# Polysketch attention and a mixture of experts: the query stage in a written order, with its work spread anew over the engines

## The chip, the core and the metric

The kernel runs on one core of a Trainium2 chip. A core has TensorE (matrix multiplies, into the PSUM memory of eight banks), VectorE and ScalarE (element by element, both read SBUF and PSUM), GpSimd (element by element in SBUF only) and SyncE, whose queue issues most of the DMA transfers. Each engine runs its own instructions in order. The metric is the device time of one execution in microseconds. In the profile's tables PE is TensorE, PEld its weight loads, DVE VectorE, ACT ScalarE, POOL GpSimd, SP SyncE.

## The reference

Attention with a polynomial sketch, 4 batches, 4 heads, 1088 positions, 32 dimensions, is followed by a two-level mixture of experts on the 4352 tokens of 128 dimensions:

```python
def phi(x):                                   # r = 8: 64 features per head
    a = einsum('rd,bhsd->bhsr', S1, x)
    b = einsum('rd,bhsd->bhsr', S2, x)
    return einsum('bhsi,bhsj->bhsij', a, b).reshape(*x.shape[:-1], r * r)
q_p, k_p = phi(q), phi(k)
kv  = einsum('bhsf,bhsd->bhfd', k_p, v)       # numerator's matrix
num = einsum('bhsf,bhfd->bhsd', q_p, kv)
den = einsum('bhsf,bhf->bhs', q_p, k_p.sum(2))[..., None] + 1e-06
x   = (num / den)                             # -> (4352, 128), heads side by side
g_logits = x @ w_group                        # argmax: group, then expert in it
e_logits = x_g @ w_expert[g]
out = g_w * e_w * (relu(x @ w1[g, e]) @ w2[g, e])
```

The denominator can come close to zero and the choice of an expert hangs on the quotient, so the kernel computes the denominator much more exactly than in fp32.

## The kernel before

**Stages.** First the k stage, batch by batch: k is cut into four bf16 slices, their products give the Gram matrix of k, which small steps (`refine`) turn into the matrix M; beside it the features of k times v give KV. Then the query stage, the part that is changed: nine units of four token tiles of 128 (the last has two). Then the routing stage, on VectorE for the most part: gates from the logits `lg`, and a sort of the tokens by expert, whose slots are computed by the matmuls `slot`. Last the expert stage, blocks of 128 tokens gathered by indirect DMA, two layers of fp32 matmuls, scattered to the output.

**The order of work.** Outside the expert stage a scheduler of the framework places the instructions on each engine; only the expert stage stands in `manual_schedule`, which keeps the written order on every engine. A pool's tile with `bufs=n` has n buffers, and an instruction that writes a buffer waits for the last readers of its former content.

**A unit of the query stage before** has two halves, written one unit apart:

- `features` (line 386 on). VectorE cuts q into four bf16 slices `qs` (`grid`, line 113: add a large constant and subtract it again, which rounds), GpSimd subtracts each slice from the rest `rq` (line 398). The four `products` per tile (line 139) multiply slice i by the first 4 - i orders of M (256, 192, 128, 64 columns) and add by order into PSUM `py`, two tiles at a time in two buffers. VectorE turns the four orders into three parts a1, a2, a3 (seven operations of 128 elements for each half of the unit), and GpSimd multiplies the parts of the two factors (eleven operations of 128 elements, lines 426 and 429) into `pr_`. Separately TensorE computes `ab` from q in fp32 (line 450, four tiles of 512 columns in three buffers, each in two instructions), ScalarE copies one factor to `ra` (line 453), and VectorE multiplies the other by it to `qp` (line 123).
- `quotient` (line 458 on). VectorE sums `pr_` to the denominator and takes the reciprocal `rec`; TensorE multiplies `qp` with KV into `pnum` (line 477, 64 columns for each pair of heads, 16 instructions in a unit); VectorE multiplies by `rec` to `xt`, which goes to DRAM as `x_d`. Then `xt` is transposed on TensorE (`px`, line 488), copied by ScalarE, multiplied with the router's weights `wr` (`pl`, line 493, 20 columns) and copied to `lg` (line 495).

## Time and profile before

| | |
|---|---|
| median of 3 runs | 468.19 us (466.86 to 469.38) |
| the profiled execution | 467.57 us, span 465.7 us, mean granted TensorE clock 0.773 |
| TensorE busy | 362.4 us (78%), weight loads 299.8 us |
| VectorE, GpSimd, ScalarE busy | 248.1, 205.9, 64.7 us |
| HBM | 29.00 MB read, 4.85 MB written |

The span is the time between the first and the last recorded instruction of the profiled execution; its own time holds some 1.9 us more. Busy time is summed over the whole span, over stages with different limits, so the tables by stage count for more. The clock is a share of 2.4 GHz: 0.50 is 1.2 GHz. Matmuls that follow each other overlap, so the time of one is read from the distance between the starts, not from its duration.

### The profile page before, as it was taken

How to read it: one execution, taken by the hardware profiler on the slowest of the kernel's cores; microseconds unless marked ns; L12 is line 12 of the kernel's file. 1: busy time of each engine (PE TensorE's matmuls, PEld its weight loads, DVE VectorE, ACT ScalarE, POOL GpSimd, SP SyncE). 2: the span in 40 equal slices, each digit the busy share in tenths (PEclk: the TensorE clock that was granted, in tenths of full speed). 3: DMA queues.
4: the chain of work that ended last, by engine and by line, in shares of the span. 5: the costliest groups of instructions: out<-in, count | busy, mean ns of one | idle time of the engine just before them, and what ended most of it. 6: DMA issues, size and time to landing. Idle time of an engine off the chain costs nothing.

```text
span 465.7 us, 6912 instructions
## 1 busy us (share of the span) xinstructions
PE 362.4 (78%) x2445; PEld 299.8 (64%) x2445; DVE 248.1 (53%) x750; ACT 64.7 (14%) x96; POOL 205.9 (44%) x248
## 2 busy tenths in 40 slices
PE   0428996972689998999959206599999999999970
PEld 0416884861253463774838106499999999999970
DVE  8698446176774575665563799323333333333320
ACT  1000000000101111111101100032222232222220
POOL 0472255100173675654653000436665556566660
PEclk9999597995665556555555556689999999999995
DMA  7991087029600000000001000101111111111120
GB/s 300 394 291 28 23 265 226 1 62 414 247 2 1 23 24 0 23 24 23 23 1 45 12 1 0 30 15 36 31 38 34 30 34 36 33 39 34 34 38 3
DMA packets 16101, 33.95 MB, mean 73 GB/s; under 512 B 2229, under 2 KB 6593, under 8 KB 16064
## 3 DMA queue, kind: packets, MB, share of 16 engines
q1 hardware_dynamic: 13376, 28.35, 17.9%
q0 software_dynamic: 2688, 5.12, 4.2%
q8 instruction: 22, 0.36, 0.3%
q14 instruction: 15, 0.12, 0.1%
HBM read 29.00 MB, written 4.85 MB: 73 GB/s over the span
## 4 chain that ended last, share of the span: by engine, by line
PE 54%; DVE 20%; issue 11%; POOL 9%; DMA 2%; ACT 0%; SPq 0%; POOLq 0%; DVEq 0%; ACTq 0%
PE ph L693 12%; PE py L699 11%; PE ab L450 9%; PE pnum L477 5%; PE py L139 4%; PE pg L305 3%; PE pl L493 3%; POOL xg L670 3%; PE slot L642 2%; POOL rk L300 2%; DVE ks L113 2%; PE px L488 1%; POOL rq L398 1%; DVE top_p_k L91 1%; DVE kp L326 1%
## 5 line engine op out<-in xcount | busy, mean ns | idle before, releaser
L693 PE MATMUL ph<-xb,w1b 128*128 128x128 f32 x656 | 82.5, 281 | 0.0
L693 PEld LDWEIGHTS ph<-xb,w1b 128*128 128x128 f32 x656 | 79.3, 198 | 0.0
L699 PE MATMUL py<-W,hT 128*128 x640 | 78.0, 275 | 0.0
L704 POOL DMA_INDIRECT out_dram<-yo,idx_s x40 | 53.2, 1331 | 49.3 <-DVE yo L702 31.4
L699 PEld LDWEIGHTS py<-W,hT 128*128 128x128 f32 x640 | 74.6, 192 | 0.0
L670 POOL DMA_INDIRECT xg<-x_d,idx_g x44 | 43.7, 992 | 52.2 <-DVE idx_s L521 39.1
L695 ACT ACTIVATE hT<-ph 128x1024 f32<-128x1024 f32 x41 | 42.0, 1023 | 143.2 <-PE ph L693 135.2
L450 PE MATMUL ab<-qT,SR 64*128 64x512 f32 (+1 forms) x72 | 54.8, 1007 | 0.1
L305 PE MATMUL pg<-ks 128*128 128x512 bf16 (+3 forms) x144 | 33.3, 349 | 16.8 <-DVE ks L113 16.8
L702 DVE TENSOR_SCALAR yo<-py,wslot 128x128 f32<-128x128 f32 x40 | 14.0, 351 | 59.9 <-PE py L699 52.5
L139 PEld LDWEIGHTS <-qs 128*128 128x128 bf16 (+1 forms) x144 | 14.9, 137 | 34.7 <-DVE qs L113 12.0
L680 DVE COPY w1b<-W 128x1024 f32 x42 | 29.4, 700 | 8.3 <-DVE yo L702 5.0
L139 PE MATMUL py<-M,qs 128*128 128x256 bf16 (+6 forms) x144 | 25.1, 323 | 9.3 <-DVE qs L113 6.7
L398 POOL TENSOR_TENSOR rq<-qT,qs 128x512 f32<-128x512 f32 (+1 forms) x9 | 10.1, 1123 | 49.0 <-DVE qs L113 42.4
L477 PE MATMUL pnum<-KV,qp 128*128 128x64 f32 (+1 forms) x144 | 30.7, 395 | 0.0
L477 PEld LDWEIGHTS pnum<-KV,qp 128*128 128x128 f32 (+1 forms) x144 | 28.8, 304 | 2.3 <-issue 1.5
L687 DVE COPY xb<-pt 128x128 f32<-128x128 f32 x42 | 12.2, 291 | 33.8 <-PE pt L686 29.6
L113 DVE TENSOR_SCALAR qs<-rq,CQ 128x512 bf16<-128x512 f32 (+1 forms) x27 | 17.1, 632 | 21.9 <-POOL rq L398 21.9
L305 PEld LDWEIGHTS <-ks 128*128 128x128 bf16 x144 | 14.7, 112 | 21.4 <-issue 18.6
L300 POOL TENSOR_TENSOR rk<-rk,ks 128x1152 f32<-128x1152 f32 x8 | 19.6, 2446 | 19.2 <-DVE ks L113 7.1
L450 PEld LDWEIGHTS ab<-qT,SR 64*128 64x128 f32 x72 | 16.7, 299 | 12.4 <-issue 7.0
L300 POOL TENSOR_TENSOR rk<-kn,ks 128x1152 f32<-128x1152 f32 x4 | 10.1, 2522 | 29.1 <-DVE pw L100 16.3
(313 smaller groups left out, 491.6 us busy)
## 6 DMA issues: line engine op xcount, KB each, us to landing
W<-in_w_dram SPq DMA_DIRECT2D x4, 2048.0 KB, 12.4
kn<-in_kn_dram SPq DMA_DIRECT2D x4, 576.0 KB, 5.3
kT<-in_kT_dram SPq DMA_DIRECT2D x4, 576.0 KB, 6.5
vn<-in_vn_dram SPq DMA_DIRECT2D x4, 576.0 KB, 3.9
qT<-in_qT_dram SPq DMA_DIRECT2D x4, 544.0 KB, 11.6
x_d<-xt SPq DMA_DIRECT2D x8, 256.0 KB, 2.3
xg<-x_d,idx_g POOLq DMA_INDIRECT x44
out_dram<-yo,idx_s POOLq DMA_INDIRECT x40
```

The lines of the kernel that those rows point to most:

```text
L113: nc.vector.tensor_scalar(out=out, in0=in_, scalar1=c, scalar2=c, op0=ALU.add, op1=ALU.subtract)
L139: nc.tensor.matmul(out(i), lhsT=left(i), rhs=right(NS - i), start=(i == 0), stop=(i == NS - 1), skip_group_check=True)
L300: nc.gpsimd.tensor_tensor(out=r, in0=rest, in1=ks[:, i], op=ALU.subtract)
L305: nc.tensor.matmul(pg[:, i:NS, :], lhsT=ks[:, i, c, :], rhs=ks[:, 0:NS - i, c, :], start=(c == 0 and i == 0), stop=(c == SC - 1 and i == N ...
L450: nc.tensor.matmul(ab[x][:, 0:w], lhsT=SR[rows, x].rearrange("p a x y -> p (a x y)"), rhs=qf[rows], start=True, stop=True)
L477: nc.tensor.matmul(pnum[r0:r0 + n, c, 64 * pr:64 * pr + 64], lhsT=qp[:, pr, cols], rhs=KV[:, b, pr, :], start=True, stop=True)
L670: nc.gpsimd.indirect_dma_start(out=xg(b), out_offset=None, in_=x_d, in_offset=bass.IndirectOffsetOnAxis(ap=idx_g[:, b:b + 1], axis=0))
L680: nc.vector.tensor_copy(out=w1b(b), in_=W1[:, ds(ex[b], 1), :].rearrange("p o f -> p (o f)"))
L693: nc.tensor.matmul(ph(b)[:, f], lhsT=w1b(b)[:, 128 * f:128 * f + 128], rhs=xb(b), start=True, stop=True)
L695: nc.scalar.activation(out=hT(b), in_=ph(b), func=ACT.Relu)
L699: nc.tensor.matmul(py(b), lhsT=hT(b)[:, f], rhs=W2[:, ds(ex[b] * FC + f, 1), :].rearrange("p o d -> p (o d)"), start=(f == 0), stop=(f == ...
L704: nc.gpsimd.indirect_dma_start(out=out, out_offset=bass.IndirectOffsetOnAxis(ap=idx_s[:, b:b + 1], axis=0), in_=yo(b), in_offset=None, bou ...
```

## The change

The query stage is written anew, under `manual_schedule`: each engine issues in the written order, in which the stages of three units interleave.

- **Slices of q.** The first two slices come from ScalarE (`act_grid`: two ACTIVATEs with a per-partition bias, +c and -c), the third is a ScalarE copy, the fourth is GpSimd's last subtraction. The slices of units 0 to 2 are issued ahead of the first matmul, those of later units two or three units ahead.
- **Orders.** One PSUM tile `py` for four tiles of tokens, in one buffer, with three orders in place of four (the last two added by TensorE). Seven matmuls per tile in place of four, 640 columns as before. M's layout has the factor ahead of the head.
- **Parts.** ScalarE rounds the first (`parts_a`), VectorE does five operations on the whole unit (256 elements per partition), into one tile `pp`.
- **Products.** GpSimd has one add and two wide multiplications, VectorE reduces the seven products to three sums.
- **spread, copy_a, features.** The four `ab` tiles have a buffer each; ScalarE copies one factor into `qp`, and VectorE multiplies in place.
- **Logits.** After the k stage, KVX is built per batch: KV beside KV times the router's weights (a transpose and a matmul on TensorE, copies on ScalarE). The numerator then has 52 columns per head, 104 per instruction, and carries the logits; `divide` multiplies both parts by `rec` and sums the heads' logits into `lg` on VectorE. The transposes `px`, the matmuls `pl` and their two ScalarE copies are gone.
- **Smaller.** wr is loaded ahead of qT, M is cleared by GpSimd instead of VectorE, there are seven small grids in place of six. The pools have one buffer unless stated.

```diff
@@ k stage
-    M = kept("M", [128, B, NS, H, 2 * R], BF16)
-    nc.vector.memset(M, 0.0)
+    KVX = kept("KVX", [128, B, H, D + NL])
+    M = kept("M", [128, B, NS, 2, H, R], BF16)
+    nc.gpsimd.memset(M, 0.0)
+        nc.sync.dma_start(out=wr, in_=wr_d)
...
-        nc.sync.dma_start(out=wr, in_=wr_d)
+        wrh = kbig.tile([128, H, NL], F32, name="wrh")
+        nc.gpsimd.memset(wrh, 0.0)
+        for h in range(H):
+            rows = slice(32 * h, 32 * h + 32)
+            nc.gpsimd.tensor_copy(out=wrh[rows, h], in_=wr[rows])
+        for b in range(B):
+            kvt = kps.tile([128, 256], F32, name="kvt", tag="small")
+            nc.tensor.transpose(kvt[:, 0:128], KV[:, b].rearrange("p a d -> p (a d)"), ident)
+            kvT = kin.tile([128, 128], F32, name="kvT")
+            nc.scalar.copy(kvT, kvt[:, 0:128])
+            kvw = kps.tile([128, 256], F32, name="kvw", tag="small")
+            nc.tensor.matmul(kvw[:, 0:H * NL], lhsT=kvT, rhs=wrh.rearrange("p h n -> p (h n)"),
+                             start=True, stop=True)
+            nc.scalar.copy(KVX[:, b, :, 0:D], KV[:, b].rearrange("p a (x d) -> p (a x) d", x=2))
+            nc.scalar.copy(KVX[:, b, :, D:], kvw[:, 0:NL * H].rearrange("p (h n) -> p h n", h=H))
@@ query stage: features() and quotient() removed, in their place
+        def act_grid(out, in_, c, cn):
+            t = qp_.tile([128, 512], F32, name="tq")[:, 0:in_.shape[1]]
+            nc.scalar.activation(out=t, in_=in_, func=ACT.Identity, bias=c)
+            nc.scalar.activation(out=out, in_=t, func=ACT.Identity, bias=cn)
+        def slice0(z, c0, nt, w):
...
+            act_grid(z["qs"][0], z["q"], CQ[:, 0:1], CQn[:, 0:1])
+        def rest1(z, c0, nt, w):
...
+            nc.gpsimd.tensor_tensor(out=z["r1"], in0=z["q"], in1=z["qs"][0], op=ALU.subtract)
+        def slice2(z, c0, nt, w):
+            nc.scalar.copy(z["qs"][2], z["r2"])
+        def slice3(z, c0, nt, w):
+            nc.gpsimd.tensor_tensor(out=z["qs"][3], in0=z["r2"], in1=z["qs"][2], op=ALU.subtract)
+        def orders(z, c0, nt, w):
+            z["py"] = qps.tile([128, 4, 4, 2 * H * R], F32, name="py")
...
+                    plan = [(0, 0, 0, 3), (0, 2, 3, 1), (1, 1, 0, 2), (1, 2, 2, 1), (2, 2, 0, 1),
+                            (2, 2, 1, 1), (3, 2, 0, 1)]
+                    for k, (i, o, j, m) in enumerate(plan):
+                        nc.tensor.matmul(z["py"][r0:r0 + n, c, o:o + m, :], lhsT=z["qs"][i][:, cols],
+                            rhs=M[:, b, j:j + m].rearrange("p j x h r -> p j (x h r)"),
+                            start=(k == 0), stop=(k == len(plan) - 1), skip_group_check=True)
+        def parts_a(z, c0, nt, w):
...
+            nc.scalar.activation(out=t, in_=z["y"][0], func=ACT.Identity, bias=CA[:, 0:1])
+            nc.scalar.activation(out=z["out"][0], in_=t.rearrange("p t (x c) -> p t x c", x=2),
+                                 func=ACT.Identity, bias=CAn[:, 0:1])
+        def parts(z, c0, nt, w):
...
+            nc.vector.scalar_tensor_tensor(out=r, in0=z["ty"], scalar=CA[:, 0:1], in1=y[0],
+                                           op0=ALU.subtract, op1=ALU.subtract)
+            sub(r, y[1], r)
+            grid(out[1], r4, CA[:, 1:2])
+            sub(r4, r4, out[1])
+            add(out[2], y[2].rearrange("p t (x c) -> p t x c", x=2), r4)
+        def multiply(z, c0, nt, w):                    # GpSimd, n = 32 nt
+            nc.gpsimd.tensor_tensor(out=pp[:, 6], in0=pp[:, 5], in1=pp[:, 3], op=ALU.add)
+            nc.gpsimd.tensor_tensor(out=g[:, 4:7], in0=pp[:, 0:1].to_broadcast([128, 3, n]),
+                                    in1=pp[:, 3:6], op=ALU.mult)
+            nc.gpsimd.tensor_tensor(out=g[:, 0:4].rearrange("p (a c) n -> p a c n", a=2), ...)
+        def spread(z, c0, nt, w):                      # ab: a PSUM bank for each of the four
+        def copy_a(z, c0, nt, w):                      # ScalarE: qp <- ab[0]
+        def features(z, c0, nt, w):                    # VectorE: qp <- ab[1] * qp
+        def numerator(z, c0, nt, w):
+            z["pn"] = qps.tile([128, 4, 256], F32, name="pn")
...
+                        k = 2 * (D + NL)
+                        nc.tensor.matmul(z["pn"][r0:r0 + n, c, k * pr:k * pr + k], lhsT=z["qp"][:, pr, cols],
+                                         rhs=KVX[:, b, 2 * pr:2 * pr + 2].rearrange("p h n -> p (h n)"),
+                                         start=True, stop=True)
+        def denominator(z, c0, nt, w):
...
+            for i, s in ((2, g[:, 1:5]), (1, g[:, 0:7:6])):
+                nc.vector.tensor_reduce(out=o[i], in_=s.rearrange("p s n r -> p n s r"), axis=AX.XY, op=ALU.add)
+            nc.vector.tensor_reduce(out=o[0], in_=g[:, 5], axis=AX.X, op=ALU.add)
+            add(o[1], o[1], o[2])
+            add(o[0], o[0], o[1])
...
+        def divide(z, c0, nt, w):
...
+            mul(xt, pn[:, :, :, 0:D], rec.to_broadcast([128, nt, H, D]))
+            nc.sync.dma_start(out=x_d[...], in_=xt.rearrange("p t h d -> p t (h d)"))
+            mul(lw, pn[:, :, :, D:], rec.to_broadcast([128, nt, H, NL]))
+            nc.vector.tensor_reduce(out=lg[:, c0:c0 + nt], in_=lw.rearrange("p t h n -> p t n h"),
+                                    axis=AX.X, op=ALU.add)
+        with tc.manual_schedule():
+            for u in range(3):
+                slice0(u)
+                rest1(u)
+                if u < 2:
+                    slice1(u)
+                    rest2(u)
+                    slice2(u)
+                    slice3(u)
+            orders(0)
+            for i in range(len(units) + 1):
+                parts_a(i)
+                parts(i)
+                slice1(i + 2)
+                spread(i)
+                copy_a(i)
+                rest2(i + 2)
+                denominator(i - 1)
+                features(i)
+                numerator(i - 1)
+                multiply(i)
+                slice2(i + 2)
+                slice3(i + 2)
+                slice0(i + 3)
+                rest1(i + 3)
+                divide(i - 1)
+                orders(i + 1)
```

## Rows read from the trace of the kernel before

**Rows 1.** Page, the span in 40 equal slices: granted TensorE clock, tenths.

```profile
PEclk9999597995665556555555556689999999999995
```

**Rows 2.** Windows by stage: microseconds and instructions per engine, granted clock, DMA share, GB/s.

```profile
core 0: us, PE busy (x) PEld busy (x) DVE busy (x) ACT busy (x) POOL busy (x), PEclk, DMA share, GB/s
0.00:124.05 124.05, 75.64 (x580) 60.05 (x581) 83.99 (x302) 5.75 (x18) 33.75 (x34) 0.84 0.62 211
124.05:259.65 135.60, 122.88 (x457) 77.01 (x454) 77.29 (x227) 16.38 (x35) 75.23 (x130) 0.55 0.06 17
```

**Rows 3.** Chain of waits, query stage's head and end: start, microseconds, what.

```profile
124.06 0.56 DVE qs L113
...
131.27 1.35 PE py L139 x10
...
259.46 0.20 ACT lg L495
```

**Rows 4.** Timeline of TensorE at 1.2 GHz: start, microseconds together, instruction.

```profile
121.72 0.33 PEld L450 LDWEIGHTS ab<-qT,SR 64*128 64x128 f32 x1 [0.51 <-issue]
...
122.57 0.33 PEld L450 LDWEIGHTS ab<-qT,SR 64*128 64x128 f32 x1 [0.52 <-issue]
...
134.56 3.67 PE L477 MATMUL pnum<-KV,qp 128*128 128x64 f32 x16
...
141.87 0.93 PE L139 MATMUL py<-M,qs 128*128 128x256 bf16 x4
...
147.06 1.35 PE L139 MATMUL py<-M,qs 128*128 128x64 bf16 x10
...
158.82 1.11 PE L488 MATMUL px<-ident,xt 128*128 128x128 f32 x4
...
169.19 1.84 PE L493 MATMUL pl<-wr,xT 128*128 128x20 f32 x8
```

**Rows 5.** Windows chosen for TensorE's clock, columns as in rows 2.

```profile
132.00:159.50 27.50, 27.50 (x67) 12.06 (x65) 15.49 (x48) 2.34 (x4) 16.96 (x28) 0.50 0.03 10
...
178.50:182.00 3.50, 3.50 (x7) 1.52 (x8) 3.50 (x15) 0.58 (x1) 2.12 (x5) 0.50 0.00 0
182.50:185.50 3.00, 1.86 (x7) 0.60 (x6) 0.76 (x3) 0.58 (x1) 2.84 (x6) 1.00 0.00 0
...
284.50:287.90 3.40, 3.40 (x17) 3.40 (x17) 2.42 (x10) 0.00 (x0) 0.00 (x0) 0.50 0.00 0
288.10:293.00 4.90, 4.90 (x46) 4.90 (x45) 3.69 (x16) 0.00 (x0) 0.00 (x0) 1.00 0.00 0
```

**Rows 6.** Groups by line and form, query stage: count, busy, mean ns.

```profile
L398 POOL TENSOR_TENSOR rq<-rq,qs 128x512 f32<-128x512 f32 x16 | 18.7, 1167 | 3.4 <-DVE qs L113 3.4
...
L123 DVE TENSOR_TENSOR qp<-ab,ra 128x512 f32<-128x512 f32 x16 | 10.8, 678 | 2.5 <-PE pnum L477 1.4 <-PE ab L450 1.1
...
L453 ACT COPY ra<-ab 128x512 f32<-128x512 f32 x15 | 8.8, 586 | 52.1 <-PE ab L450 46.0 <-DVE qp L123 6.1
...
L467 DVE TENSOR_SCALAR den<-den,scale 128x16 f32<-128x16 f32 x8 | 3.2, 396 | 0.0
...
L123 DVE TENSOR_TENSOR qp<-ab,ra 128x256 f32<-128x256 f32 x2 | 0.8, 382 | 0.0
```

**Rows 7.** The same view, VectorE's reduces, contiguous and strided.

```profile
L461 DVE TENSOR_REDUCE dn<-pr__1556 128x48 f32<-128x384 f32 x1 | 0.5, 547 | 0.0
...
L524 DVE TENSOR_REDUCE ez<-sel 128x136 f32<-128x544 f32 x1 | 1.0, 983 | 0.0
```

**Rows 8.** Timeline, VectorE beside GpSimd in the k stage.

```profile
25.63 2.43 POOL L300 TENSOR_TENSOR rk<-rk,ks 128x1152 f32<-128x1152 f32 x1 [1.70 <-DVE s1s L113]
25.76 2.32 DVE L117 TENSOR_TENSOR r<-r,s1s 128x8 f32<-128x8 f32 x1
...
31.00 0.14 DVE L117 TENSOR_TENSOR r<-r,s1s 128x8 f32<-128x8 f32 x1
```

More of the change, by code (lines that the diff above doesn't have):

```diff
@@ new lines, in parts @@
+        @staged
+        def parts(z, c0, nt, w):
+            y, out = z["y"], z["out"]
+            r = qp_.tile([128, 4, 2 * H * R], F32, name="rest")[:, 0:nt]
+            r4 = r.rearrange("p t (x c) -> p t x c", x=2)
+            nc.vector.scalar_tensor_tensor(out=r, in0=z["ty"], scalar=CA[:, 0:1], in1=y[0],
[4 more added lines that the diff above has]
+            add(out[2], y[2].rearrange("p t (x c) -> p t x c", x=2), r4)
@@ new lines, in spread @@
+        @staged
+        def spread(z, c0, nt, w):
+            z["ab"] = [[qps.tile([128, 512], F32, name=f"ab{x}{pr}")[:, 0:w] for pr in range(2)]
+                       for x in range(2)]
+            for x in range(2):
+                for pr in range(2):
+                    rows = slice(64 * pr, 64 * pr + 64)
+                    nc.tensor.matmul(z["ab"][x][pr], lhsT=SR[rows, x].rearrange("p a x y -> p (a x y)"),
+                                     rhs=z["q"][rows], start=True, stop=True)
@@ L487, in quotient @@
-            for c in range(nt):
-                nc.tensor.transpose(px[:, 128 * c:128 * c + 128], xt[:, c, :], ident)
-            xT = qp_.tile([128, 512], F32, name="xT", bufs=1)
-            nc.scalar.copy(xT[:, 0:w], px[:, 0:w])
-            pl = qps.tile([128, 4, NL], F32, name="pl")
-            for c in range(nt):
-                nc.tensor.matmul(pl[:, c], lhsT=xT[:, 128 * c:128 * c + 128], rhs=wr, start=True,
-                                 stop=True)
-            nc.scalar.copy(lg[:, c0:c0 + nt], pl[:, 0:nt])
```

184 lines of the change are left out of this document (84 added, 100 removed).

## The prediction, on record before the result was seen

> **What bounds the kernel now.** I read the page's slices first: from about a quarter to two thirds of the span the granted TensorE clock stands mostly at 5 tenths [rows 1]. The windows by stage put a number on it: the query stage, from 124.05 to 259.65 us, is 135.6 of the 465.7 us of the span. TensorE is busy in 122.9 of it, but at a mean clock of 0.55; VectorE is busy 77.3, GpSimd 75.2, ScalarE 16.4 [rows 2]. The chain of waits shows how the stage begins and ends: the first slice qs at 124.06, then a ladder of VectorE and GpSimd slices, the order matmuls of unit 0 only at 131.27, and the last copy of the logits at 259.46, which releases the routing stage [rows 3]. Inside, the chain is almost all TensorE. So the stage is bound by TensorE at 1.2 GHz, and 7 us at its head by the slices.
>
> The run of a unit (four tiles) on TensorE at 1.2 GHz, from the timeline [rows 4]: the two weight loads of ab that follow each other start 0.85 us apart (121.72, 122.57), and a unit has eight ab instructions: 6.8. The 16 numerator matmuls take 3.6. Per tile the four order matmuls go from 0.23 (four wide ones in 0.93) to 0.135 (ten of 64 columns in 1.35): 0.23 + 0.2 + 0.165 + 0.135, four times, 2.9. Transposes px 1.1, logits pl 1.8. Sum 16.2; by 8.5 units 138, against 135.6 for the stage. The sum holds, so I use these prices.
>
> **The clock** decides most, and I take it from windows only [rows 5]. From 132 to 159.5 us TensorE shows 27.5 us busy of 27.5 and runs at 0.50 throughout. It came up to 1.00 after an unbroken stretch of ab (178.5 to 182, then 1.00 at 182.5), and lost it again when the next slices were late and TensorE was busy only 1.86 of 3.0 us. The slot matmuls of the routing stage (98 columns per load) also lifted it: 0.50 in 284.5 to 287.9, 1.00 from 288.1. There 17 matmuls in 3.4 us become 46 in 4.9: 0.20 us to 0.107, so the whole TensorE price halves.
>
> **TensorE after, per unit.** spread is the same eight instructions, now issued in one row with four tiles of their own, no longer broken by waits for a free ab buffer: 6.8. numerator is 16 matmuls of 104 columns in place of 64. At 64 columns the weight load sets the pace (0.225 each); the 98-column slot matmuls run at 0.20, so the added columns hide behind the load: 3.6, and if they don't, 104/64 of it, 5.9, as the upper bound (2.3 more on a round at 1.2 GHz, within the range). orders has seven matmuls per tile in place of four for the same 640 columns: 0.23 + 0.17 + 5 x 0.135 = 1.07, four times, 4.3. px and pl go: -2.9. With three changes of kind at some 0.15 each: 15.1 at 1.2 GHz, 7.6 at 2.4. At the low clock that is only 1.1 us less than the 16.2 of today.
>
> **VectorE after, per unit** [rows 6, 7]. parts: five operations of 256 elements at 0.382 (the 256-wide qp), 1.9, in place of 14 small ones. denominator: reduces of 512, 256 and 128 elements; 384 contiguous ones took 0.55 and 544 strided ones 0.98, so about 0.70 + 0.42 + 0.28; two adds, the scalar step and the reciprocal, all four at the 0.40 of the scalar step, which holds waits: 3.0. features 2 x 0.68. divide: xt like qp 0.68, the logit product of 320 elements between 0.38 and 0.68, 0.46, its reduce 0.48: 1.6. Sum 7.9. The four slices leave VectorE.
>
> VectorE also waits for GpSimd. A subtraction of 8 elements took 2.32 us beside a GpSimd operation and 0.14 without one [rows 8]. About six operations of a unit have such inputs: in denominator the adds and the scalar step, whose price of 0.40 already holds it, and grid and sub of parts, which run while rest2 does; I give those two a third of a GpSimd subtraction each, 0.8: 8.7. The Trainium skill, SBUF — State Buffer, section Who interferes with whom, says that VectorE instructions with two SBUF inputs, or in a two-port mode, and GpSimd lock each other out for a whole instruction. The rows agree in kind. Taken in full, with each of six instructions behind a GpSimd subtraction of 1.17, that rule would give 7.9 + 7.0 = 14.9 in place of 8.7; that is a rival below.
>
> **ScalarE and GpSimd.** ScalarE gets nine operations of 512 elements: at the 0.586 of a plain copy 5.3 per unit. Six of them have a bias operand, of which no row shows the price: nothing more at the one end, at the other a whole further copy each, 5.3 + 3.5 = 8.8. I take the plain copy, since the same elements pass; either end leaves P at or near VectorE's 8.7. The Trainium skill, ScalarE: Activation LUTs, section What ACT_TABLE_LOAD costs, prices such an operand so that 512 elements take 0.71; by that ScalarE has 6.0, and the bound does not move. GpSimd: three subtractions and the product of 512 elements at 1.17, the product of 384 and the add, three quarters and a quarter of the elements, at most 1.17 together: 5.9, in place of three subtractions and eleven small operations [rows 6]. Neither sets the pace.
>
> **Does the written order hold back TensorE?** orders(i+1) needs py free, which parts(i) ends: two ScalarE operations 1.2 to 1.4, five of VectorE 2.0, together 3.5 after orders(i). Spread and numerator cover 5.2 of TensorE even at 2.4 GHz. Behind the waiting parts_a on ScalarE stand slice1 and copy_a; copy_a is due only after spread (3.4 or more). features(i) waits for copy_a, and numerator(i) is a whole round later. So a round P is the larger of TensorE and VectorE: 8.7 where the clock stays up, 15.1 where it never rises, 10.1 where TensorE spends half of its time at each level (mean rate 0.75). At P near 9 TensorE idles one or two us in a round, which is the state in which the rows show the clock lost; but each spread at 1.2 GHz is 6.8 us of unbroken ab, which the rows show to lift it. I take between the two: 9.5.
>
> **Stage and ends.** orders(0) can start when M is written, since slices of units 0 and 1 no longer need M, VectorE or the time after 124: 4.3 at the low clock, parts_a 1.4, eight rounds, then the half unit's rest (parts 1.5, denominators 3.0 and 1.8, features 0.8, divides 1.6 and 0.9: 9.6). 4.3 + 1.4 + 9.6 = 15.3, and 15.3 + 8 x 9.5 = 91.3; against 135.6 that is -44.3.
>
> **Ahead of the stage.** VectorE's chain of small operations that makes M runs to 124.05. Into it come: KVX (per batch a transpose, two matmul passes, three ScalarE copies; ScalarE idles there, but the PSUM buffers "small" are shared with that chain), and seven GpSimd subtractions of 1.17 for units 0 to 2, which can lock VectorE out. Nothing to 6 us; I take 2.5, since most gaps on GpSimd lie earlier. One small grid more and the M memset, which leaves VectorE for GpSimd at the kernel's start, are within that. wr's load moves ahead of the four of qT on SP's queue, so qT lands later by one small transfer; p_q, which reads it, is needed only by the slices, and the whole k stage covers that; without the cover it is one issue. The writes of x_d stay one per unit. Routing and expert stages are untouched: their first lg read moves with the stage.
>
> Sum: 467.57 (the profiled execution; span 465.7 plus 1.9 around it, and 0.6 under the median of 468.19) - 44.3 + 2.5 = 425.8: **426 us**.
>
> **Rivals.** (a) The clock stays up once risen and VectorE alone sets P at 7.9 to 8.5: 15.3 + 63 to 68, so 410 to 418 with 0 to 2.5 ahead. For: spread and numerator are denser than today; against: each round has idle TensorE. Chance 0.20. (b) The clock is mostly low, P 11 to 14: 438 to 462. For: 132 to 159.5, fully busy at 0.50. Chance 0.13. (c) It never rises: P 15.1, 15.3 + 120.8 = 136.1, and 470.6 with the 2.5: at the edge of no change. Against: the unbroken ab of 178.5. Chance 0.05. (d) VectorE behind GpSimd in full: P 14.9, by the same sum 469. Against: the means in the trace hold far smaller waits. Chance 0.03. (e) Slower: the 64-column matmuls, three more loads per tile, pay 0.23 each instead of 0.135 while the clock is low; orders 6.2, P 17.0, and 15.3 + 1.9 + 136.0 - 135.6 + 2.5 make +20.1: 488. It decides from P over 14.7, where (135.6 - 2.5 - 15.3)/8 is used up. Against: ten of them took 1.35. Chance 0.04. The forecast, P 8.5 to 11 and 418 to 438, has 0.55.
>
> **Chances and range.** A difference of 0.5% (2.3 us) is about what this measurement can tell from none. Faster: 0.55 + 0.20 + 0.13 and a little of the edge, 0.89; within 0.5%, (d) and half of (c): 0.06; slower, (e) and the rest of (c): 0.05. For 8 in 10 the range goes from the low end of (a), with nothing ahead, TensorE's own P of 7.6 and orders(0) at 2.4 GHz (13.2 + 60.8 = 74.0, 406), into (b) as far as P 12.5 with 5 ahead: 15.3 + 100 = 115.3, 452.
>
> **What would show it.** TensorE's row in the query stage: clock over 0.7 on average, ab in rows of eight at 0.43 to 0.85 each, the first py within 1 us of the M copy. VectorE nearly closed (over 80%) if (a) or the forecast holds, half idle if (b) or (c). numerator at more than 0.23 each at 1.2 GHz would refute the hidden columns. A VectorE operation of over 1 us beside GpSimd points to (d); M later than 127 us refutes the term ahead. The prediction is wrong if the clock neither rises nor falls as I read it, for 7 us per round hang on that.

## The result: 420.84 us, and the profile after

The changed kernel takes 420.84 us (median of 4 runs, 419.52 to 422.11) against 468.68 us of the kernel before on the same chip: ratio 0.898 (95% interval 0.894 to 0.903). The forecast was 426 us (406 to 452), faster. The profiled execution took 419.52 us, 48.05 less than the one of before.

The windows by stage of the kernel after, then stretches inside its query stage (columns as in [rows 2]):

```profile
0.00:130.97 130.97, 74.86 (x585) 60.48 (x585) 88.20 (x302) 16.49 (x41) 43.58 (x47) 0.81 0.59 200
130.97:212.05 81.08, 62.15 (x468) 42.46 (x468) 73.47 (x153) 37.96 (x69) 44.42 (x51) 0.84 0.10 27
...
131.10:133.30 2.20, 2.19 (x28) 2.09 (x28) 0.00 (x0) 0.00 (x0) 0.00 (x0) 0.50 0.03 7
133.40:137.05 3.65, 3.65 (x9) 1.12 (x9) 2.16 (x5) 3.28 (x6) 1.09 (x1) 0.51 0.01 2
158.16:186.70 28.54, 22.98 (x170) 15.56 (x168) 27.71 (x52) 16.09 (x29) 17.84 (x19) 0.83 0.10 28
```

The query stage has gone from 135.60 us [rows 2] to 81.08, that is -54.5 where -44.3 was forecast; M came at 130.97 us in place of 124.05, +6.9 where +2.5 was forecast. The routing and expert stages changed by 0.4 us together. In the stage TensorE is busy 62.15 us where it was 122.88; VectorE is busy 73.47 where it was 77.29. So TensorE's busy time was halved, part of it by the higher clock, and VectorE's hardly changed. The rounds start (first operation of `parts`) at 133.94, 139.54, 149.29, 158.16, 167.68, 177.19, 186.70, 195.50 and 203.18: 2.97 from M to the first, 69.24 for eight rounds, 8.87 behind the last start. The last line above is three rounds of 9.51 us, in which VectorE is busy 27.71 of 28.54.

The page's slices of the kernel after, against [rows 1]: in the stage the clock has come up from mostly 5 to mostly 8 and 9, and VectorE's row shows the stage as a block of nines.

```profile
DVE  8699736527675799999999952333333333333320
PEclk9999879797555996988855597999999999999995
```

VectorE's groups in the stage (columns as in [rows 6]), and one round of the timeline, VectorE beside GpSimd:

```profile
L123 DVE TENSOR_TENSOR qp<-ab,qp 128x512 f32<-128x512 f32 x16 | 9.8, 657 | 1.0 <-PE ab L516 1.0
L555 DVE TENSOR_SCALAR o<-o,scale 128x16 f32<-128x16 f32 x8 | 8.2, 1024 | 0.3
L120 DVE TENSOR_TENSOR o<-o,o 128x16 f32<-128x16 f32 x16 | 7.9, 497 | 0.3
...
L113 DVE TENSOR_SCALAR pp<-rest,CA 128x256 f32<-128x256 f32 x8 | 5.4, 681 | 0.3
```

```profile
158.93 1.16 POOL L442 TENSOR_TENSOR r<-r,qs 128x512 f32<-128x512 f32 x1 [1.65 <-ACT qs L421]
159.12 1.11 DVE L113 TENSOR_SCALAR pp<-rest,CA 128x256 f32<-128x256 f32 x1
...
162.18 1.19 DVE L120 TENSOR_TENSOR o<-o,o 128x16 f32<-128x16 f32 x2
162.34 1.00 POOL L501 TENSOR_TENSOR g<-pp 128x384 f32<-128x384 f32 x1 [0.66 <-DVE o L120]
163.30 1.26 POOL L503 TENSOR_TENSOR g<-pp 128x512 f32<-128x512 f32 x1
163.41 1.19 DVE L555 TENSOR_SCALAR o<-o,scale 128x16 f32<-128x16 f32 x1
...
187.67 0.41 DVE L113 TENSOR_SCALAR pp<-rest,CA 128x256 f32<-128x256 f32 x1
```

The scalar step on 16 elements costs 1.02 us, more than a multiplication of 512. In the timeline it, an addition and the grid each lie over a running GpSimd operation and end with it; the grid of 187.67, with GpSimd idle, takes 0.41. This is what [rows 8] showed, at the places where the prediction expected it, but longer than it was priced.

### The profile page after: what moved, and what is told of

Its sections match the earlier page's. It is cut to its first block, busy times and chain, and to the rows that moved or that the text cites. A ratio compares the mean times of both kernels' runs of the same rounds, so it can differ in the third digit from the quotient of the medians.

```text
span 417.7 us, 6896 instructions
## 1 busy us (share of the span) xinstructions
PE 300.2 (72%) x2463; PEld 264.9 (63%) x2463; DVE 248.1 (59%) x676; ACT 97.1 (23%) x153; POOL 182.2 (44%) x182
## 3 DMA queue, kind: packets, MB, share of 16 engines
q0 software_dynamic: 2688, 5.12, 4.9%
## 4 chain that ended last, share of the span: by engine, by line
PE 46%; DVE 34%; issue 8%; POOL 4%; DMA 3%; ACT 1%; SPq 0%; DVEq 0%; POOLq 0%
PE ph L791 16%; PE py L797 15%; PE pg L309 4%; PE pv L339 3%; POOL rk L304 2%; PE slot L740 2%; DVE ks L113 2%; DVE o L555 2%; DVE o L550 2%; DVE o L120 2%; DVE rest L117 2%; DMA out_dram<-yo,idx_s 2%; DVE qp L123 1%; DVE lg L572 1%; DVE pp L113 1%
## 5 line engine op out<-in xcount | busy, mean ns | idle before, releaser
L802 POOL DMA_INDIRECT out_dram<-yo,idx_s x40 | 50.1, 1252 | 51.7 <-DVE yo L800 27.1
L516 PE MATMUL ab<-qT,SR 64*128 64x512 f32 (+1 forms) x72 | 26.8, 728 | 7.7 <-DVE qp L123 7.6
L539 PEld LDWEIGHTS pn<-KVX,qp 128*128 128x128 f32 (+1 forms) x144 | 19.6, 225 | 11.0 <-issue 5.7
L539 PE MATMUL pn<-KVX,qp 128*128 128x104 f32 (+1 forms) x144 | 21.9, 326 | 4.4 <-DVE lw L123 4.4
L339 PE MATMUL pv<-vn,kp 128*128 128x64 f32 x144 | 22.9, 325 | 0.0
L339 PEld LDWEIGHTS pv<-vn,kp 128*128 128x128 f32 x144 | 22.1, 240 | 0.2
L442 POOL TENSOR_TENSOR r<-r,qs 128x512 f32<-128x512 f32 (+1 forms) x9 | 9.9, 1102 | 27.9 <-ACT qs L421 27.9
L304 POOL TENSOR_TENSOR rk<-kn,ks 128x1152 f32<-128x1152 f32 x4 | 10.1, 2525 | 27.2 <-DVE pw L100 15.1
L463 PE MATMUL py<-M,qs 128*128 128x64 bf16 (+5 forms) x252 | 15.0, 226 | 8.8 <-DVE pp L120 5.4
L463 PEld LDWEIGHTS <-qs 128*128 128x128 bf16 (+1 forms) x252 | 13.8, 112 | 11.5 <-DVE pp L120 6.2
```

The lines of the kernel that those rows point to most:

```text
L304: nc.gpsimd.tensor_tensor(out=r, in0=rest, in1=ks[:, i], op=ALU.subtract)
L339: nc.tensor.matmul(pv[:, 64 * pr:64 * pr + 64], lhsT=kp[:, j, 2 * pr:2 * pr + 2, :].rearrange("p h f -> p (h f)"), rhs=vn[b][:, j, 64 * pr ...
L463: nc.tensor.matmul(z["py"][r0:r0 + n, c, o:o + m, :], lhsT=z["qs"][i][:, cols], rhs=M[:, b, j:j + m].rearrange("p j x h r -> p j (x h r)") ...
L516: nc.tensor.matmul(z["ab"][x][pr], lhsT=SR[rows, x].rearrange("p a x y -> p (a x y)"), rhs=z["q"][rows], start=True, stop=True)
L539: nc.tensor.matmul(z["pn"][r0:r0 + n, c, k * pr:k * pr + k], lhsT=z["qp"][:, pr, cols], rhs=KVX[:, b, 2 * pr:2 * pr + 2].rearrange("p h n ...
L802: nc.gpsimd.indirect_dma_start(out=out, out_offset=bass.IndirectOffsetOnAxis(ap=idx_s[:, b:b + 1], axis=0), in_=yo(b), in_offset=None, bou ...
```

## The experiments

The theory going in: VectorE sets the round, some 2 us of it being waits for GpSimd, and the 6.9 us ahead are split between KVX in TensorE's order and GpSimd's slices beside the chain that makes M. The rivals: TensorE and its clock set the round; or one of the two is the whole loss ahead. All runs are compared with the kernel before on the same chip; M is the end of its last copy, the stage runs from there to the first read of all logits. These two and the round are read from one execution of each kernel; a range of rounds leaves out the first and the last. The five kernels that start alike (after, e3, e4, e6, e9) have M from 130.09 to 131.55, so a difference of 1 us in M is no effect of an edit.

| | median us | ratio to before, 95% | M us | stage us | steady round us |
|---|---|---|---|---|---|
| after | 420.84 | 0.898 (0.894 to 0.903) | 130.97 | 81.1 | 9.51 |
| e4_orders_twice | 423.60 | 0.906 (0.903 to 0.909) | 130.09 | 83.3 | 9.51 |
| e3_den_adds_gpsimd | 414.59 | 0.885 (0.880 to 0.890) | 131.37 | 74.3 | 8.66 |
| e6_operand_in_psum | 427.29 | 0.913 (0.910 to 0.916) | 131.55 | 87.6 | 8.2 to 10.6 |
| e9_parts_psum_only | 410.68 | 0.878 (0.875 to 0.881) | 131.29 | 69.7 | 7.65 |
| e1_kvx_last | 427.76 | 0.915 (0.912 to 0.918) | 123.20 | 94.9 | 9.51 |
| e2_quiet_gpsimd | 418.05 (one run) | | 127.23 | 81.0 | 9.51 |
| e7_short_lead | 421.81 | 0.901 (0.897 to 0.905) | 125.44 | 87.0 | 9.51 |
| e8_psum_and_short_lead | 430.58 | 0.918 (0.914 to 0.922) | 126.60 | 94.8 | 8.1 to 10.4 |
| e5_logits_by_transpose | 412.78 | 0.882 (0.879 to 0.885) | 126.20 | 77.6 | 7.85 |
| e10_transposes_and_psum | 410.18 | 0.874 (0.868 to 0.880) | 129.99 | 72.6 | 6.3 to 9.5 |
| e12_planned_order | 423.20 | 0.906 (0.904 to 0.909) | 127.83 | 86.4 | 7.0 to 10.7 |
| e13_slices_on_vector | 427.41 | 0.915 (0.912 to 0.917) | 127.92 | 90.5 | 9.6 |

### Which engine sets the round

**Double TensorE's orders.**

```diff
-                    for k, (i, o, j, m) in enumerate(plan):
+                    for k, (i, o, j, m) in 2 * list(enumerate(plan)):
```

> Edit: the 28 matmuls of the orders of every unit run twice, the second pass overwriting the first with the same values; nothing is left out. It adds 28 x 8.5 = 238 matmuls at 0.047 (full clock) to 0.082 us (half clock), 11 to 19 us of TensorE's time, to a stage of 81 us in which TensorE is busy for 62. Theory (VectorE sets the round): most of it is hidden, the stage grows by under 3 us beyond the first pass of unit 0 (2 us), the kernel 420 to 424. Rival 1 (TensorE sets the round): plus 11 to 19 us, 430 to 438. Rival 2 (a busier TensorE holds its full clock and this shortens the round): the granted clock goes from 0.84 to over 0.9 and the kernel is not slower.

The same three rounds in this run's windows:

```profile
159.45:187.99 28.54, 22.39 (x256) 15.97 (x255) 27.71 (x52) 16.09 (x29) 17.84 (x19) 1.00 0.10 29
```

256 matmuls in place of 170, a clock of 1.00 in place of 0.83, and the three rounds take the same 28.54 us with the same 27.71 of VectorE. So neither TensorE's load nor its clock sets this round; VectorE does. The stage grew by 2.2 us, of which 2.15 lie ahead of the first `parts` (135.21 - 130.09 = 5.12 against 2.97), where unit 0's orders are waited for. Rival 2 has the clock right (0.91 over the stage), and the higher clock buys nothing.

**Take the waits off VectorE, first by moving them.**

```diff
-            add(o[1], o[1], o[2])
-            add(o[0], o[0], o[1])
-            nc.vector.tensor_scalar(out=o[0], in0=o[0], scalar1=scale, ...)
+            nc.gpsimd.tensor_tensor(out=o[1], in0=o[1], in1=o[2], op=ALU.add)
+            nc.gpsimd.tensor_tensor(out=o[0], in0=o[0], in1=o[1], op=ALU.add)
+            nc.gpsimd.tensor_scalar(out=o[0], in0=o[0], scalar1=scale, ...)
```

> Edit: in the denominator the two additions and the scalar step on 128x16 elements go from VectorE to GpSimd, and the reciprocal moves from the denominator into the divide, behind the features; nothing is left out. Theory: VectorE sets the round of 9.5 us, and these three operations take 2.0 us of it (2 x 0.497 + 1.024) because each waits for a running GpSimd operation; without them the round is 7.5 to 7.8 us, the stage 81 - 8.5 x 1.8 = 66 us, the kernel 404 us (400 to 409). Rival 1 (TensorE and its clock set the round, VectorE only fills it): the round stays 9.5 and the kernel 419. Rival 2 (the wait moves to the next VectorE operation that meets GpSimd, the reciprocal or the grid step): these grow by 0.5 to 1 us each, the gain is under 6 us, 414 to 419.

The round fell by 0.85 us, not 1.8. VectorE's groups of this run show where the rest went:

```profile
L117 DVE TENSOR_TENSOR rest<-rest,pp 128x256 f32<-128x256 f32 x6 | 6.2, 1037 | 0.2
L113 DVE TENSOR_SCALAR pp<-rest,CA 128x256 f32<-128x256 f32 x6 | 4.9, 817 | 0.2
```

The subtraction `rest<-rest,pp`, 0.53 us in the kernel after, now lies beside a GpSimd subtraction and takes 1.04. Rival 2 was half right: the wait moved to the next operation with all operands in SBUF.

**Then by keeping one operand in PSUM.** The second remainder goes into columns of `py` that are free, the sum of the second order into free columns of `pn`:

```diff
-            sub(r, y[1], r)
-            grid(out[1], r4, CA[:, 1:2])
-            sub(r4, r4, out[1])
+            sub(d, y[1], r)                       # d = py[:, 0:nt, 3, :]
+            grid(out[1], d4, CA[:, 1:2])
+            sub(r4, d4, out[1])
...
+            o[1] = z["pn"][:, 0, 240:240 + nh]    # pn allocated in denominator()
```

> Edit: nothing moves between engines and no operation is added; in the parts the second remainder, and in the denominator the sum of the second order, are kept in columns of PSUM that the tiles py and pn leave free, so that every addition, subtraction, grid and scalar step of VectorE reads at most one operand from SBUF; nothing is left out. Theory: VectorE sets the round, and 2.0 to 2.6 us of it are waits for a running GpSimd operation, which only its operations with all operands in SBUF suffer (rows with a PSUM operand take 0.42 us in every round); these return to 0.16 to 0.42 us, the round goes from 9.4 to 7.2 to 7.5 us, the kernel to 402 to 405 us. Rival 1 (what was seen with the additions on GpSimd: the wait is only passed on to the next operation): a reduce, reciprocal or multiplication grows by about 1 us instead, round over 9, kernel 416 to 420. Rival 2 (with VectorE at 7.3, TensorE's 62 us of work and its clock take over): VectorE idles behind TensorE, the granted clock goes under 0.8, round 8 to 9, kernel 408 to 415.

The kernel became slower, by a wait that none of the three named. The timeline of this run:

```profile
172.06 1.00 POOL L503 TENSOR_TENSOR g<-pp 128x384 f32<-128x384 f32 x1
...
172.11 0.18 DVE L120 TENSOR_TENSOR pn<-o,pn 128x16 f32<-128x16 f32 x1
...
172.32 0.23 DVE L558 TENSOR_SCALAR o<-pn,scale 128x16 f32<-128x16 f32 x1
...
172.70 3.20 PE L540 MATMUL pn<-KVX,qp 128*128 128x104 f32 x16 [2.98 <-DVE o L558]
...
175.94 0.69 DVE L123 TENSOR_TENSOR xt<-pn,rec 128x512 f32<-128x512 f32 x1 [1.96 <-PE pn L540]
```

The scalar step is down to 0.23 and the second addition to 0.18, while GpSimd runs its multiplication `g` beside both, as the theory has it. But now the numerator's matmuls wait 2.98 us for VectorE's last read of a sum that shares their tile, the orders stand behind them in TensorE's order, and VectorE then idles 1.96 before `xt`. So the sum was put into the next unit's `py` instead:

```diff
-            o[1] = z["pn"][:, 0, 240:240 + nh]
+            o[1] = live.get(c0 // 4 + 1, z)["py"][:, 0, 3, 0:nh]
```

> Edit: as with both operands in PSUM, but the sum of the denominator stands in free columns of the next unit's py instead of pn, so that the numerator's matmuls no longer follow the denominator; nothing is left out. Theory: in the run with pn the waits behind GpSimd did go (scalar step 0.23 against 1.13 us, additions 0.17 against 0.51, grid 0.54 against 0.76) and the round still was 9.5, because the numerator waited 2.9 us a round for the denominator that shares its bank and the orders stood behind it; with that new wait away the round falls to VectorE's own 7.2 to 7.8 us, the kernel to 403 to 408 us. Rival 1 (TensorE, with 62 us of work at the clock it is granted, is the bound as soon as VectorE is under 9 us): round 8.5 to 9.5, clock under 0.8, kernel 414 to 422. Rival 2 (the orders now wait for the denominator in py and take the place of the numerator's wait): TensorE idles before py for over 1 us a round, kernel 410 to 420.

Three rounds in this run's windows, and its groups of VectorE:

```profile
147.51:170.46 22.95, 15.98 (x160) 11.64 (x160) 21.48 (x52) 15.71 (x28) 18.00 (x19) 0.95 0.13 36
```

```profile
L558 DVE TENSOR_SCALAR o<-py,scale 128x16 f32<-128x16 f32 x6 | 1.4, 234 | 0.2
L120 DVE TENSOR_TENSOR py<-o,py 128x16 f32<-128x16 f32 x6 | 1.1, 178 | 0.2
L120 DVE TENSOR_TENSOR py<-py,o 128x16 f32<-128x16 f32 x6 | 1.0, 172 | 0.0
```

The same 52 operations over three rounds take 21.48 us busy in place of 27.71, and the round is 7.65 in place of 9.51. Nothing moved between engines: 2.08 us of every round were waits for GpSimd, and all of that but 0.2 comes back as time. In this run GpSimd mostly idles during the additions and the scalar step (in one round from 157.58 to 159.22), so a part of the gain is that they no longer meet it; the run with `pn` shows that they are as short beside it. The kernel is 10 us faster than the change, but 3 us over the theory's 403 to 408: the first round stays at 5.6 us, and the one of 7.68 falls to 7.2 only. The Trainium skill, SBUF — State Buffer, section Who interferes with whom, says that a VectorE instruction with at most one SBUF input, outside the two-port modes, does not contend with GpSimd. The rows agree: with `pn`, 0.18 and 0.23 us beside a running GpSimd operation.

### What came ahead of the stage

The timeline of the kernel after, from the last batch of the k stage to the first slice:

```profile
101.53 0.28 DVE L91 TENSOR_REDUCE m_ref<-t_g 128x1 f32<-128x128 f32 x1
...
103.80 0.43 ACT L345 COPY KV<-pv 64x64 f32<-64x64 f32 x2 [4.21 <-PE pv L339]
104.27 0.48 PE L359 MATMUL kvt<-ident,KV 128*128 128x128 f32 x1 [0.51 <-ACT KV L345]
...
105.61 0.42 PE L96 MATMUL pw_t<-ident,m_ref 128*1 128x128 f32 x1
...
106.07 0.28 DVE L91 TENSOR_REDUCE top<-pw_t 1x1 f32<-1x128 f32 x1 [4.06 <-PE pw_t L96]
...
107.50 0.16 DVE L107 TENSOR_SCALAR p_g<-pw_t 128x1 f32<-128x1 f32 x1 [0.74 <-PE pw_t L105]
107.53 1.15 POOL L433 TENSOR_TENSOR r<-qT,qs 128x512 f32<-128x512 f32 x1 [24.55 <-ACT qs L421]
...
107.89 0.88 DVE L281 TENSOR_SCALAR t_g<-t_g,inv_ref 128x128 f32<-128x128 f32 x1
```

m_ref is there at 101.8, but its transpose stands behind the last `pv` and KVX's `kvt` in TensorE's order, and VectorE waits 4.06 us. Then the chain's small operations meet GpSimd's subtractions. Two runs take one of the two away.

```diff
+        (the loop that builds KVX, moved behind this line)
         Ns, p_n = refine([pn[:, i] for i in range(NS)], B * R, "n")
```

> Edit: the loop that builds KVX (four transposes, products and copies) is written behind the last refinement of the M chain instead of ahead of the first one; nothing is left out. Theory: of the 6.9 us by which M came later (130.97 against 124.05 us), about 2.9 are TensorE's transpose for the scale p_g standing behind KVX's transposes and the last key and value product, so p_g comes near 104.6 to 105.0 us instead of 107.50, M near 128 us, the stage stays 81 us, and the kernel gains about 2.9 us (416.6). Rival 1: the whole 6.9 us come from the slices that GpSimd computes beside the chain: p_g and M stay where they are, no gain (419.5). Rival 2: the whole of it is KVX: M back at 124, 412.6 us.

```diff
-            nc.gpsimd.tensor_tensor(out=z["r1"], in0=z["q"], in1=z["qs"][0], op=ALU.subtract)
+            nc.scalar.copy(z["r1"], z["q"])       # r2 and qs3 likewise, units 0 to 2 ahead only
```

> Edit: the eight GpSimd subtractions that slice units 0 to 2 ahead of the stage become plain ScalarE copies, so that GpSimd does nothing beside the chain that makes M (the remainders of these units are wrong, their number and sizes stay). Theory: about 4.0 of the 6.9 us are small VectorE operations of the chain that waited for a GpSimd subtraction (0.87 to 1.21 us where they took about 0.3); they return to about 0.3 us, M comes near 127 us, the kernel gains 4 us (415.5). Rival 1 (all of the loss is KVX): M stays at 131, no gain. Rival 2 (the small operations are slow for another reason, such as ScalarE's copies): the operations stay near 1 us with GpSimd silent.

The timelines, first with KVX last, then with GpSimd silent:

```profile
103.79 0.16 DVE L107 TENSOR_SCALAR p_g<-pw_t 128x1 f32<-128x1 f32 x1 [0.73 <-PE pw_t L105]
...
122.42 0.78 DVE L380 COPY M<-s_n 32x128 bf16<-32x128 bf16 x4
...
139.55 0.48 DVE L485 SCALAR_TENSOR_TENSOR rest<-ty,CA,py 128x256 f32<-128x256 f32 x1 [16.34 <-ACT ty L475]
```

```profile
107.83 0.16 DVE L107 TENSOR_SCALAR p_g<-pw_t 128x1 f32<-128x1 f32 x1 [0.73 <-PE pw_t L105]
...
108.22 0.28 DVE L281 TENSOR_SCALAR t_g<-t_g,inv_ref 128x128 f32<-128x128 f32 x1
...
126.45 0.78 DVE L391 COPY M<-s_n 32x128 bf16<-32x128 bf16 x4
```

With GpSimd silent, p_g to M takes 127.23 - 107.83 = 19.40 us against 130.97 - 107.50 = 23.47: the slices cost 4.07, and the operation on t_g is back from 0.88 to 0.28. With KVX last, p_g comes 3.7 us earlier. A part of that goes with the clock: from 98 to 101 us, at the last `pv`, it was 0.74 in the kernel after and 1.00 in this run. In the run with the orders doubled, which has KVX ahead, it was 1.00 too, and p_g came at 106.64. Here the forecast of the run failed: the slices themselves, which stand behind KVX's copies in ScalarE's order, began only at 125.6, ran behind M instead of beside the chain, and the first `parts` came 5.6 us later than in the kernel after. That is why M at 123.20 goes with 427.76 us: the 14 us from the first slice to the first `parts` have to lie beside the chain for the most part, even if the slices slow it by 4.

```diff
-            for u in range(3):     # slice0, rest1 of units 0 to 2, the rest of units 0 and 1
...
+            for step in (slice0, rest1, slice1, rest2, slice2, slice3):
+                step(0)
+            slice0(1)
+            rest1(1)
+            logit_values()         # KVX, all batches in one tile of pn
             orders(0)
...
-                slice1(i + 2)
+                slice1(i + 2 if i else 1)    # round 0: all that is left of units 1 and 2
```

> Edit: KVX is built at the stage's head (in the numerator's bank, batches together) behind the slices, and only unit 0 and the first subtraction of unit 1 are sliced ahead; the rest of units 1 and 2 goes into round 0; nothing is left out. Theory: the loss of 6.9 us is KVX (3.7) ahead of p_g and GpSimd's eight subtractions (4.06) beside the chain from p_g to M (23.47 us here, 19.43 before and 19.41 with GpSimd silent); with KVX away from the front and four subtractions left M comes at 125 to 126 us, the first parts 3 us later, round 0 1 to 3 us longer: 414.5 to 417. Rival (the slices of unit 1 are then late and the second round waits for them): what M gains is lost in round 0, 418 to 421.

M came at 125.44, as expected; but the second round began at 141.51 (139.54 after), because unit 1's slices were now in round 0. The rival holds: the gain of 5.5 us went there. This trade of latency for latency is worth nothing.

### The other parts of the change

**Logits by transposes, as before, within the written order** (`pl` stands in `px`'s bank, KVX and its loop are gone):

```diff
-            mul(lw, pn[:, :, :, D:], rec.to_broadcast([128, nt, H, NL]))
-            nc.vector.tensor_reduce(out=lg[:, c0:c0 + nt], in_=lw.rearrange("p t h n -> p t n h"), ...)
...
+                turn_x(i - 2)      # PE: px[:, 128 * c:] <- transpose of xt[:, c]
+                copy_x(i - 2)      # ScalarE: xT <- px
...
+                logits(i - 2)      # PE: px[:, NL * c:] <- xT, wr
...
+                copy_l(i - 2)      # ScalarE: lg <- px
```

> Edit: within the new order the logits go back to transposes of x, a ScalarE copy, four products with the router's weights and a copy, two rounds later; KVX and its four transposes are gone, the numerator has 64 columns; nothing is left out. Theory: carrying the logits costs VectorE two operations a round (0.48 + 0.70 us) and KVX delays M by 3.7 us (p_g at 107.50 against 103.79 us with KVX behind); so M near 127.3 us, the round 1.0 to 1.2 us shorter, the end longer by a turn, copy, product and copy (2 to 3 us): 406 to 410 us. Rival (what the logits cost VectorE is taken again by waits for GpSimd): round shorter by under 0.5 us, 413 to 416. Rival 2 (the change's logits are the gain: TensorE's eight more matmuls and ScalarE's two copies a round bind): 420 or more.

M is 4.8 us earlier and three rounds take 23.54 us, with 45 VectorE operations for 52:

```profile
161.80:185.34 23.54, 22.22 (x206) 16.27 (x203) 22.81 (x45) 16.72 (x34) 15.51 (x17) 1.00 0.13 35
```

So carrying the logits in the numerator cost time in this kernel, ahead of the stage by KVX and in the round: it took them off TensorE, which had room, and gave 1.2 us a round to VectorE, which had none. The median is 412.78, the round 1.66 shorter, the end longer by 3 us (203.81 - 191.89 = 11.9 behind the last start, against 8.9). The theory's sum of 406 to 410 was 3 us too low: two rounds, of 8.6 and 10.2 us, lie ahead of the short ones.

**No written order.**

```diff
-        with tc.manual_schedule():
+        if True:
```

> Edit: the query stage is no longer issued in the written order; the planner orders the same instructions on every engine as it did in the kernel before; nothing is left out. Theory (the gain is VectorE's work per unit, from 16.0 us busy to 8.6 us a unit, and an order only has to keep it fed): VectorE is still the bound, round 9.5 to 11, stage 81 to 95, kernel 420 to 434. Rival (the written order is what keeps TensorE from standing behind waits, and its clock up): the granted clock of the stage falls to about 0.6 as in the kernel before, VectorE's busy share under 0.75, kernel 440 to 465.

```profile
127.83:214.24 86.41, 65.70 (x462) 45.27 (x459) 63.43 (x153) 42.23 (x78) 52.73 (x58) 0.78 0.11 31
```

Without the written order the stage is 5.3 us longer, M 3.1 earlier, the kernel 2 to 4 us slower, so the gain of 48 does not hang on the order. The loss is at the head: the first `parts` comes 9.26 us behind M in place of 2.97, since the slices now stand behind the chain, while the eight rounds take 67.8 us in place of 69.24. The theory's total came true, but not its reason. VectorE's work per unit did not fall from 16.0 us busy to 8.6: the 16.0 is the time of the stage per unit, and VectorE was busy 77.29 us in it, 9.1 per unit. In this run it is busy 63.43 us of 86.41, less than the 0.75 that the rival named, at a clock of 0.78; what bounds its rounds is not shown.

**Grids of the slices on VectorE.**

```diff
-            nc.scalar.activation(out=t, in_=in_, func=ACT.Identity, bias=c)
-            nc.scalar.activation(out=out, in_=t, func=ACT.Identity, bias=cn)
+            grid(out, in_, c)
```

> Edit: the two grid steps per unit of the query slices go back from two ScalarE activations each to one VectorE operation each, in the same written places; nothing is left out. Theory (VectorE sets the round): two operations of 0.41 to 0.55 us alone, with operands all in SBUF, so each may wait up to 1.16 us for a GpSimd subtraction: plus 0.9 to 3 us a round, 8 rounds, and 1 to 4 us ahead of the stage, 428 to 446. Rival (the slices were a latency and not VectorE's load: ScalarE's 2.9 us a unit leave the chain of a unit): round within 0.5 us, kernel 417 to 424.

The stage is 9.4 us longer, the kernel 6 to 8 slower. Of it 7 lie at the head: M at 127.92 and the first `parts` at 137.87, since the slices now stand behind the chain on VectorE. The steady round is only 0.1 us longer: VectorE got two grids (1.25 and 0.54 us in that run's groups) and met GpSimd in fewer other places (the additions 0.32 us for 0.50, the grid of `parts` 0.41 for 0.68). The theory's 0.9 to 3 us a round was wrong; its total of 428 to 446 was missed by under 1 us, and came that near only by the head.

### Together

The edits of e6_operand_in_psum and of e7_short_lead in one kernel:

> Edit: the operands in PSUM and the short lead together; nothing is left out. Theory: the two gains are in different places and add: minus 15 to 17 and minus 3 to 5, 398 to 402 us. Rival: with VectorE free of the waits the slices of round 0 are on the path, and the sum is 3 us or more short.

430.58, some 10 us over the change, where the new wait for `pn` alone costs 6 and the late slices of unit 1 alone 1: the two losses add, and the theory's gains of both failed.

The edits of e5_logits_by_transpose and of e9_parts_psum_only in one kernel, and at the end:

```diff
+                if i == len(units):
+                    numerator(i - 1)         # ahead of the turn of x
                 turn_x(i - 2)
```

> Edit: logits by transposes of x (as in the run before) together with the operands in py's free columns, and for the last unit the numerator stands ahead of the turn of x; nothing is left out. Theory: VectorE has 1.2 us a round less than in the run with the operands alone, so its own time is 6.0 to 6.3 us, and something else binds the round: TensorE's 7.6 us at full clock or the chain of one unit; round 6.8 to 7.8, kernel 397 to 404 us. Rival (a busier TensorE falls to its lower clock and sets a round of 8 or more): 408 to 414.

Two rounds of this run in the windows:

```profile
154.37:163.83 9.46, 8.40 (x70) 6.80 (x68) 5.91 (x15) 5.95 (x11) 7.81 (x8) 0.76 0.11 28
...
171.47:178.13 6.66, 6.66 (x75) 5.29 (x73) 5.91 (x15) 5.40 (x11) 5.01 (x6) 1.00 0.06 16
```

VectorE has the same 5.91 us in both, and is no longer the bound: the round is 6.66 at a clock of 1.00, with TensorE busy throughout, and 9.46 at 0.76, with TensorE busy 8.40. So here TensorE and its clock set the round, as the prediction had thought of the change itself, and the rival's 408 to 414 came true. Its median of 410.18 is within the spread of the 410.68 with the operands in PSUM alone; both beat the change by 10 us.

## Why the prediction came out right, and where it was off

Most signs named beforehand were there: the stage's clock 0.84 (over 0.7), the first `py` at 131.11, 0.14 us after the last copy of M, VectorE busy 73.47 of 81.08 (91%). One was not: `ab` came in rows of eight in some rounds only, and at 0.25 to 0.46 us each, not 0.43 to 0.85. The sum of 425.8 against 419.5 still hides two errors of 10.2 and 4.4 us with opposite signs, and one figure that was right for the wrong reason.

- **What sets P: wrong in the mechanism.** The step "a round P is the larger of TensorE and VectorE", with 15.1 us for TensorE at 1.2 GHz, made the clock decide, and 9.5 was taken "between the two". The round is 9.51, but it is VectorE alone, the mechanism of rival (a) at a larger price, so the 9.5 was luck. The 7 us per round that were to hang on the clock did not: at 1.00 in place of 0.83 three rounds took the same 28.54 us. TensorE was over-priced. Its groups on the pages, first of the kernel before and then of the one after (columns as in [rows 6]):

```profile
L450 PE MATMUL ab<-qT,SR 64*128 64x512 f32 (+1 forms) x72 | 54.8, 1007 | 0.1
L139 PE MATMUL py<-M,qs 128*128 128x256 bf16 (+6 forms) x144 | 25.1, 323 | 9.3 <-DVE qs L113 6.7
L477 PE MATMUL pnum<-KV,qp 128*128 128x64 f32 (+1 forms) x144 | 30.7, 395 | 0.0
...
L516 PE MATMUL ab<-qT,SR 64*128 64x512 f32 (+1 forms) x72 | 26.8, 728 | 7.7 <-DVE qp L123 7.6
L463 PE MATMUL py<-M,qs 128*128 128x64 bf16 (+5 forms) x252 | 15.0, 226 | 8.8 <-DVE pp L120 5.4
L539 PE MATMUL pn<-KVX,qp 128*128 128x104 f32 (+1 forms) x144 | 21.9, 326 | 4.4 <-DVE lw L123 4.4
```

- **spread, forecast at 6.8, takes 3.65** at a clock of 0.51 (133.40 to 137.05) and 1.99 at 1.00. For the kernel before, the price of 0.85 for a row was right, and with it the unit of 16.2: by line the stage holds 51.4 us of `ab` and 25.1, 30.7, 9.5 and 15.1 of `py`, `pnum`, `px` and `pl`, 131.9 together against the forecast's 138. But the order of the instructions changed. Before, the two `ab` instructions that follow each other read the same 64 partitions of q; spread has the two loops the other way round, so neighbours read different halves. Its weight loads then come in twos, 0.85 us from pair to pair, where [rows 4] has one load each time:

```profile
134.35 0.34 PEld L516 LDWEIGHTS ab<-qT,SR 64*128 64x128 f32 x2 [0.51 <-issue]
...
135.20 0.34 PEld L516 LDWEIGHTS ab<-qT,SR 64*128 64x128 f32 x2 [0.51 <-issue]
```

These loads show that two rows run beside each other. That the order of the loops brings it about is argued, since no run turned them back.
- **orders, forecast at 4.3, takes 2.2** at 0.50 (131.10 to 133.30). The row of ten matmuls in [rows 4] names the form of its first alone: by form they are four of 64 columns and two each of 256, 192 and 128. So 0.135 was a mean over all widths, and the narrow matmuls that the change adds cost far less.
- **numerator's added columns are hidden, as forecast:** at 0.50 the twelve loads with 104 columns take 2.64 us, the sixteen with 64 columns before 3.48, that is 0.22 each in both.

```profile
158.60 2.64 PEld L539 LDWEIGHTS pn<-KVX,qp 128*128 128x128 f32 x12 [0.25 <-issue]
...
134.55 3.48 PEld L477 LDWEIGHTS pnum<-KV,qp 128*128 128x128 f32 x16 [1.50 <-issue]
```

- **TensorE in sum:** 3.65 + 16 x 0.22 + 2.2 = 9.4 us at 1.2 GHz where 15.1 was forecast and 16.2 is the unit before, and 1.99 + 2.00 + 1.31 = 5.3 at 2.4. This is a little under VectorE's 9.5 at the low level and far under it at the high one. So the stage became shorter because TensorE fell below VectorE; what each part of that is worth is not shown, as no run gives TensorE its old work back.
- **VectorE, 7.9 + 0.8.** Measured 7.16 of its own (21.48 / 3 with the operands in PSUM) and 2.08 of waits: sum 9.24, and 0.27 idle. The waits were under-priced: 0.8 for them, and about 0.6 that the three prices of 0.40 held (the two additions and the scalar step take 0.58 together with an operand in PSUM), make 1.4. In the kernel after the three hold 2.0 us together. Taken in full for six instructions (rival (d), 14.9) the waits would have been over-priced: about three of them meet a GpSimd operation in a round.
- **Head, rounds and end.** 4.3 + 1.4 to the first `parts` was 2.97; eight rounds were 69.24 and not 76, since the first (5.60, no unit before it to divide) and the last two (8.80 and 7.68, with half a unit or none left to slice) are short and were counted as full; the end was 8.87 for 9.6. Together -10.2.
- **Ahead of the stage, 2.5 with a bound of 6.** Measured 6.9, above the bound, and "M later than 127 us refutes the term ahead" applies. KVX holds back p_g by about 2.9 (107.50 against 104.62 before), through TensorE's order, with the lower clock in it, and not through the PSUM buffers named: `pw_t` follows KVX's matmuls with no idle time of TensorE before it. The seven slices on GpSimd cost 4.07. The 2.5 was to cover both.
- **ScalarE** did not set the pace, as forecast: it is busy 37.96 of 81.08 us. The ACTIVATE with a bias takes 0.72 us for 512 elements in the trace, so the plain copy's 0.586 was low. The Trainium skill, ScalarE: Activation LUTs, section What ACT_TABLE_LOAD costs, gives a price from which 0.71 follows as an estimate; the rows agree.

## What to carry to other kernels

Find the engine that is busy throughout the stage after a change, not the one before: here TensorE gave way to VectorE, and work that left TensorE for VectorE (the logits) then cost time. A small VectorE operation beside busy GpSimd is priced by the GpSimd operation, not by its elements; give it one operand in PSUM, in a tile that no waiting matmul shares. A price that adds up for the old code need not hold for the new: where the order of the instructions changes, look for a stretch of the old trace that has the new order. A merged row names one form only; ask for the forms before dividing its time by its count.
